# Tile 1's loads on SyncE, matmuls of ones on TensorE, and masks on GpSimd, in a fused attention and feed-forward kernel

## The chip, the cores and the metric

The kernel runs on one core of a Trainium2 chip. The metric is the device time of one execution in microseconds (us); the median of several runs is given with its range. A run comes with a mean granted TensorE clock, 1.0 being full speed. Profiles are of one execution each; their times count from the start of the profiled span. Engines: PE is TensorE (PEld its weight loads), DVE is VectorE, ACT is ScalarE, POOL is GpSimd, SP is SyncE; a q after the name marks the engine's DMA issues.

## The reference, cut to what matters

```python
# attention: q, k, v are (4 batches, 8 heads, 768, 64) in fp32
scores = q @ k.T / sqrt(64)
# heads flagged in is_retrieval: causal mask.
# other heads: causal AND (the first 4 keys OR the last 64 keys)
a = softmax(where(mask, scores, -1e9))
x = (a @ v).transpose(0, 2, 1, 3).reshape(3072, 512)
# feed-forward
h = x @ w_in          # 512 x 2048
g = h - tanh(h)
out = g @ w_out       # 2048 x 512
```

## The kernel before

The kernel cuts the 3072 tokens into 12 tiles of 256, three per batch. For each tile it casts q, k and v to 16 bits, forms scores for pairs of heads on TensorE (`sc`), exponentials on ScalarE (`pt`), masks, the product with v (`av`), the normalised result (`x`, or `x16t` from tile 3 on), its transpose (`xT`), and then the feed-forward (`ph`, `gt`, `po`, `ot`). Tiles 0 to 2 transpose their result on TensorE; tiles from 3 on do it with DMA transposes that SyncE issues. The work of one tile is laid between that of others.

A small list scheduler in the program fixes each engine's order of instructions ahead of time, from a duration that the author gives to each operation:

```python
def op(eng, ns, fn, r=(), w=(), dma=None, prio=None, port=False, after=None, behind=None): ...

def masks(threshold, key, heads, added=False):
    for h in heads:
        ...
        op("DVE", 350,
           lambda h=h, how=how: nc.vector.tensor_scalar(
               out=m4[:, h, :], in0=A4[:].rearrange("p a c -> p (a c)"),
               scalar1=threshold[:, h : h + 1], **how),          # 128 x 512, 16 bit
           r=[key, "A4", "A40", "A41", "A43"], w=[("m4", h // 2)], port=True)
...
for half in range(2):                      # tile 0: SyncE's ring, fp32
    load(0, "qk", (half,))
    load(0, "v", (half,))
...
load_cast(1, [("rv", 0, "v", 0, 1)], "qk") # tile 1: GpSimd's casting loads
if first:
    load_w_in(*W_IN[0], ())                # weights, chunk one, in GpSimd's queue
...
if t == 1 and hp == HP - 1:                # masks of tile 2, on VectorE
    fs.append(lambda: masks(thr, "thr", range(H)))
...
def st_X_tile(t):                          # tiles from 3 on: xT by DMA
    for i in range(NB):
        op("SP", 1250, lambda i=i: nc.sync.dma_start_transpose(...),
           r=[("x16t", t)], w=[("xT", t, "all", i)], dma=(512, 22.0))
```

The softmax here doesn't subtract the row's maximum and nothing guards it: scores larger than these inputs give would overflow.

## Time and profile before

| | before |
|---|---|
| time, median of 3 runs | 238.59 us (238.48 to 238.87) |
| profiled span, mean granted clock | 236.7 us, 1.00 |
| TensorE busy | 221.5 us, 94% |
| TensorE idle before its first instruction | 6.0 us |
| first feed-forward matmul of tile 0 starts | 18.93 us |
| first evacuation of a finished output block (`ot` on ScalarE) starts | 49.89 us |
| last evacuation on ScalarE starts | 230.10 us |

The last three rows are the milestones of this document: the evacuations are the same 24 instructions in every version, so the shift of the first, the sixth or the last of them tells how much time has been won or lost by then. The prediction below shows the lines that the rest of the reading of this profile rests on.

### The profile page before, as it was taken

The page shows a single profiled execution, that of the slowest core. Times are in us where ns is not written, and L with a number is a line of the kernel's source. Part 1 is how long each engine was busy: PE and PEld are TensorE (multiplying, and loading weights), DVE is VectorE, ACT ScalarE, POOL GpSimd, SP SyncE. Part 2 cuts the span into 40 slices and gives each one's busy share as a digit, 9 for nine tenths or more (in the row PEclk, how much of TensorE's full clock was granted, in tenths as well). Part 3 has the DMA queues.
Part 4 walks back from the last instruction along what each step waited for, and adds up shares of the span by engine and source line. Part 5 has one row for each costly group of instructions (what it writes and reads, how often), then busy time and mean ns, then how long its engine had stood idle before and what let it go on. Part 6 is the DMA issues. An engine that isn't in the chain of part 4 may idle for free. (4 is left out here: it accounts for less than half of the span.)

```text
span 236.7 us, 5895 instructions
## 1 busy us (share of the span) xinstructions
PE 221.5 (94%) x2220; PEld 157.8 (67%) x2220; DVE 139.0 (59%) x343; ACT 143.6 (61%) x221; POOL 90.5 (38%) x218
## 2 busy tenths in 40 slices
PE   0889899999999999999999999999999999999991
PEld 0346687756776777777676777776776777777661
DVE  1856665864488657767666655667766546443300
ACT  3668677884588387466686649537759464444320
POOL 5999420089818068480814904606300000000000
PEclk9999999999999999999999999999999999999999
DMA  5999999999997999979989695998712101310121
GB/s 128 209 140 172 204 181 204 197 228 224 206 225 182 151 248 184 227 153 206 239 168 214 136 186 130 186 171 179 134 47 66 38 31 47 90 38 9 44 89 51
DMA packets 108130, 35.29 MB, mean 149 GB/s; under 512 B 100290, under 2 KB 104642, under 8 KB 108098
## 3 DMA queue, kind: packets, MB, share of 16 engines
q1 hardware_dynamic: 92642, 28.98, 60.5%
q0 software_dynamic: 15168, 5.77, 20.7%
q8 instruction: 18, 0.29, 0.5%
q10 hardware_dynamic: 288, 0.14, 0.2%
q14 instruction: 14, 0.11, 0.2%
HBM read 27.27 MB, written 6.29 MB: 142 GB/s over the span
## 5 line engine op out<-in xcount | busy, mean ns | idle before, releaser
L1135 PE MATMUL ph<-xT,win 128*128 128x256 f16 x768 | 101.7, 273 | 0.6 <-DMA win<-in_moe_w_in_dram 0.3
L1194 PE MATMUL po<-wout,gt 128*128 128x512 f16 (+1 forms) x400 | 98.0, 371 | 0.3 <-ACT ot L1170 0.3
L1148 ACT ACTIVATE th<-ph 128x512 f32<-128x512 f32 x96 | 57.6, 601 | 59.6 <-PE ph L1135 58.2
L1155 DVE SCALAR_TENSOR_TENSOR gt<-th,ph 128x512 f16<-128x512 f32 x96 | 65.4, 684 | 44.9 <-ACT th L1148 44.4
L1135 PEld LDWEIGHTS <-win 128*128 128x128 f16 x768 | 80.0, 114 | 13.0 <-issue 1.9
L961 ACT ACTIVATE pt<-sc 128x1024 f16<-128x1024 f32 (+1 forms) x78 | 68.5, 926 | 11.4 <-PE sc L941 10.9
L1194 PEld LDWEIGHTS <-gt 128*128 128x128 f16 x400 | 36.4, 98 | 24.6 <-issue 0.9
L680 POOL CAST t<-raw_rqk 128x256 f16 x72 | 28.5, 440 | 63.3 <-DMA raw_rqk<-in_k_dram 48.1
L1030 PEld LDWEIGHTS <-pt 128*128 128x128 f16 x552 | 25.9, 98 | 10.4 <-issue 0.9
L1030 PE MATMUL av<-v,pt 128*128 128x65 f16 x304 | 26.0, 195 | 0.1
L941 PE MATMUL sc<-qk 64*128 64x128 f16 (+1 forms) x412 | 23.8, 240 | 1.7 <-DVE qk L826 1.7
L941 PEld LDWEIGHTS <-qk 64*128 64x128 f16 x412 | 13.7, 94 | 13.5 <-issue 8.9
L675 POOL CAST v<-raw_rv 128x128 f16 x72 | 21.1, 335 | 4.2 <-DMA raw_rv<-in_v_dram 4.2
L1060 DVE TENSOR_TENSOR x16t<-av,rinv 128x128 f32 x72 | 20.8, 289 | 2.3 <-DVE rinv L1050 0.3
L1030 PE MATMUL av<-vf,pt 128*128 128x65 f16 x248 | 19.6, 193 | 0.0
L1170 ACT ACTIVATE ot<-po 128x512 f32<-128x512 f32 (+1 forms) x24 | 14.3, 596 | 8.5 <-PE po L1194 8.4
L996 DVE TENSOR_TENSOR pt<-pt,m 128x1024 f16<-128x1024 f16 x16 | 12.3, 768 | 8.0 <-ACT pt L961 8.0
L1050 DVE RECIPROCAL rinv<-av 128x4 f32<-128x4 f32 x48 | 8.6, 179 | 13.4 <-PE av L1030 13.4
L986 DVE TENSOR_TENSOR pt<-pt,mS 128x512 f16<-128x512 f16 x24 | 9.8, 449 | 6.7 <-ACT pt L961 6.7
L843 PEld LDWEIGHTS <-t 128*128 128x128 f16 x48 | 3.9, 107 | 8.9 <-ACT t L644 6.8
L523 DVE TENSOR_SCALAR m<-A,thr 128x512 f16<-128x512 f16 x16 | 7.4, 501 | 1.7 <-PE sc L928 1.2
L751 POOL TENSOR_TENSOR vf<-v,rflagr 128x260 f16<-128x260 f16 x12 | 7.5, 634 | 0.0
(95 smaller groups left out, 90.8 us busy)
## 6 DMA issues: line engine op xcount, KB each, us to landing
out_dram<-ot SPq DMA_DIRECT2D x23, 256.0 KB, 2.3
raw_rqk<-in_q_dram SPq DMA_DIRECT2D x20, 256.0 KB, 4.7
raw_rqk<-in_k_dram SPq DMA_DIRECT2D x20, 256.0 KB, 4.5
raw_rv<-in_v_dram SPq DMA_DIRECT2D x18, 256.0 KB, 4.4
win<-in_moe_w_in_dram POOLq DMA_DIRECT2D x4, 512.0 KB, 8.8
wout<-in_moe_w_out_dram POOLq DMA_DIRECT2D x4, 512.0 KB, 12.4
raw_rv<-in_v_dram SPq DMA_DIRECT2D x4, 128.0 KB, 4.7
t<-in_q_dram POOLq DMA_DIRECT2D x4, 128.0 KB, 9.5
```

The costliest lines, as they stand in the source:

```text
L675: nc.gpsimd.tensor_copy(out=v1s[b]()[:, lo : lo + NB, rank : rank + 1, 0:D], in_=raw_of("v", t)[:, :, at, :],)
L680: nc.gpsimd.tensor_copy(out=t16[t % 2][:, :, :, rank : rank + 1, :], in_=raws["rqk", t][0]()[:, :, :, at, :],)
L941: nc.tensor.matmul(out=sc()[:, hh, o : o + nb * 128].rearrange("p (i c) -> p i c", c=128), lhsT=ks.rearrange("p i c -> p (i c)")[p_, jb * ...
L961: lambda pt=pt, gi=gi, wid=wid, sc=sc: nc.scalar.activation(out=pt()[:, :, 512 * gi : 512 * gi + wid], in_=sc()[:, :, 0:wid], func=AF.Exp, ...
L996: nc.vector.tensor_mul(out=pv, in0=pv, in1=m4[:, h0 : h0 + 2, 256:512].unsqueeze(2).to_broadcast([128, 2, 2, 256]),)
L1030: nc.tensor.matmul(out=av()[:, i, hh, :], lhsT=pt()[:, hh, co : co + 128], rhs=vv, start=(jb == first_jb), stop=(jb == qb),)
L1060: nc.vector.tensor_mul(out=x16s[t]()[:, :, at, :], in0=av()[:, :, hh : hh + 1, 0:D], in1=rinv()[:, :, hh : hh + 1].unsqueeze(3).to_broadca ...
L1135: nc.tensor.matmul(out=ph()[:, j, :], lhsT=w()[:, cb, c0 + fb % 4 : c0 + 512 : 4], rhs=xTs[t]()[:, cb, :], start=(cb == 0), stop=(cb == HP ...
L1148: lambda: nc.scalar.activation(out=th()[:], in_=ph()[:], func=AF.Tanh, scale=1.0 / XS),
L1155: lambda: nc.vector.scalar_tensor_tensor(out=gts[t]()[:, u * FU : (u + 1) * FU, :], in0=th()[:], scalar=-XS, in1=ph()[:], op0=ALU.mult, op ...
L1170: nc.scalar.activation(out=ot()[:, c0:c1], in_=po()[:, c0:c1], func=AF.Copy, scale=1.0 / XS)
L1194: nc.tensor.matmul(out=po()[:, c0:c1], lhsT=gts[t]()[:, f, ts * 128 : ts * 128 + 128], rhs=w_out_t[f // 4]()[:, f % 4, c0:c1], start=(f == ...
```

## The change

It has three parts. Tile 1's q and k come by SyncE's ring as fp32 in 512 B packets instead of by GpSimd's casting loads (DMA transfers that convert to 16 bits on the way), and GpSimd casts them; the weights can then be issued earlier. TensorE multiplies ones from 1.2 us until data come, and in planned gaps of tile 0, in order that its clock goes to full speed sooner. The eight masks of tile 2 go from VectorE to GpSimd. A few constants of the scheduler's cost model change with it.

```diff
@@ the scheduler
-    def run(self):
+    def run(self, fill=None, until=None):
+            if e == "PE" and t < 5600:
+                ns *= 2
...
+                idle = self.start[i] - free
+                if self.fill and idle > 200 and i != until and self.FROM < free:
+                    self.fill(int(idle * 0.5 / 107), 256)
@@ which loads take two tokens per packet (512 B)
-            return nm != "v" and t == 0
+            return nm != "v" and t < 2 and (first or not t)
@@ the ones
+            wm, key = bank([128, 512], FP32, "o", "warm")
+            def run_up(n=10, c=512):
+                for _ in range(n):
+                    nc.tensor.matmul(out=wm()[:, 0:c]..., lhsT=ones[:], rhs=ones[:]..., start=True, stop=True)
+            op("PE", 2130, run_up, r=["ones"], w=[key])
+            fillers.append(run_up)
@@ masks
-        def masks(threshold, key, heads, added=False):
+        def masks(threshold, key, heads, added=False, eng="DVE"):
-                    "DVE", 350,
-                    lambda h=h, how=how: nc.vector.tensor_scalar(
+                    eng, {"DVE": 350, "POOL": 560}[eng],
+                    lambda h=h, how=how: engs[eng].tensor_scalar(
@@ tile 1
-        load_cast(1, [("rv", 0, "v", 0, 1)], "qk")
-            load_w_in(*W_IN[0], ())
+            load(1, "qk", (0,))
+            load(1, "qk", (1,))
+            cast_qk(1, (("POOL", "POOL"), ("POOL", "POOL")))
+            load_w_in(*W_IN[0], raw_keys("q", 0, 1))
@@ masks of tile 2
-                    fs.append(lambda: masks(thr, "thr", range(H)))
+                    fs.append(lambda: masks(thr, "thr", range(H), eng="POOL"))
```

(Cut: further constants of the scheduler, the value casts of tile 0 placed earlier in the list.)

More of the change, by code (lines that the diff above doesn't have):

```diff
@@ L24 @@
     PSUM = ("sc", "m", "h", "o")
+    FROM = 5800
     RESULT = {"PE": 200, "ACT": 0, "DVE": 0, "POOL": 0, "SP": 0}
@@ L39, in op @@
                 deps.add(self.writer[k])
-            if k[0] in self.PSUM:
+            if isinstance(k, tuple) and k[0] in self.PSUM:
                 deps.update(j for j in self.readers.get(k, ()) if self.ops[j][0] != eng)
@@ L57, in op @@
         return i
-    def run(self):
+    def run(self, fill=None, until=None):
+        self.fill = fill
         n = len(self.ops)
@@ L140, in run @@
             for u in followers[i]:
-                ready[u] = max(ready[u], t + ns)
+                ready[u] = max(ready[u], free[e])
                 left[u] -= 1
@@ L147, in run @@
                 rings["POOL" if e == "POOL" else "SP"].append(
-                    [i, t + ns + (1200 if e == "POOL" else 300), each, packets * each / 16]
+                    [i, t + ns + (1200 if e == "POOL" else 1000 if t < 6000 else 400), each, packets * each / 16]
                 )
@@ L152, in run @@
         self.end = max(self.done)
+        free = self.FROM
         for i in order:
+            if self.ops[i][0] == "PE":
+                idle = self.start[i] - free
+                if self.fill and idle > 200 and i != until and self.FROM < free:
+                    self.fill(int(idle * 0.5 / 107), 256)
+                free = max(free, self.start[i] + self.ops[i][1])
+                if i == until:
+                    self.fill = None
             self.ops[i][2]()
@@ L261, in program @@
         rot = {}
+        fillers = []
         def bank(shape, dt, tag, name):
@@ L425, in program @@
             op(
-                "ACT", 400,
+                "ACT", 1150,
                 lambda: nc.scalar.dma_start(
@@ L431, in program @@
             )
-        for half in range(2):
-            load(0, "qk", (half,))
-            load(0, "v", (half,))
+        load(0, "q", (0,))
+        load(0, "k", (0,))
+        load(0, "v", (0,))
+        load(0, "q", (1,))
+        load(0, "k", (1,))
+        load(0, "v", (1,))
         if first:
             op("POOL", 204, lambda: nc.gpsimd.memset(ones[:], 1.0), w=["ones"])
+            wm, key = bank([128, 512], FP32, "o", "warm")
+            def run_up(n=10, c=512):
+                for _ in range(n):
+                    nc.tensor.matmul(
+                        out=wm()[:, 0:c].rearrange("p (a c) -> p a c", c=128), lhsT=ones[:],
+                        rhs=ones[:].unsqueeze(1).to_broadcast([128, c // 128, 128]),
+                        start=True, stop=True,
+                    )
+            op("PE", 2130, run_up, r=["ones"], w=[key])
+            fillers.append(run_up)
             op(
@@ L879, in program @@
         first_S = {}
+        first_x = []
         def near(n):
@@ L1110, in mm @@
                     )
-            op("PE", 112, mm, r=[("x16", n), "ident"], w=[key])
+            first_x.append(op("PE", 112, mm, r=[("x16", n), "ident"], w=[key]))
             op(
@@ L1262, in program @@
         cast_qk(0, (("ACT", "ACT"), ("ACT", "DVE")), (0,))
-        load_cast(1, [("rv", 0, "v", 0, 1)], "qk")
         if first:
-            load_w_in(*W_IN[0], ())
+            load(1, "qk", (0,))
+            load(1, "qk", (1,))
+            cast_qk(1, (("POOL", "POOL"), ("POOL", "POOL")))
+        else:
+            load_cast(1, [("rv", 0, "v", 0, 1)], "qk")
+        cast_v(0, ("POOL", "POOL"), (0,))
+        cast_v(0, ("POOL", "POOL"), (1,))
+        if first:
+            load_w_in(*W_IN[0], raw_keys("q", 0, 1))
             load_cast(1, (), "v")
@@ L1270, in program @@
             masks(thr, "thr", range(2 * n, 2 * n + 2), added=True)
-            st_T(n, "ACT", "DVE")
+            st_T(n, *("ACT", "DVE"))
             for f in scores(n):
                 f()
-        cast_v(0, ("POOL", "POOL"), (0,))
         cast_qk(0, (("ACT", "ACT"), ("ACT", "DVE")), (1,))
@@ L1279, in program @@
             masks(thr, "thr", range(2 * n + 4, 2 * n + 6), added=True)
-            st_T(n + 2, "ACT", "DVE")
+            st_T(n + 2, *("ACT", "DVE"))
             for f in scores(n + 2):
@@ L1283, in program @@
             st_X(n, "o", "ACT")
-        cast_v(0, ("POOL", "POOL"), (1,))
         for n in (2, 3):
@@ L1401, in program @@
         with tc.manual_schedule():
-            P.run()
+            P.run(fillers[0] if fillers else None, first_x[0])
     program(True)
```

## The prediction

> **What bounds the kernel now.** I read the page first, then the stretches by engine, then TensorE's waits, then the timeline of the first 34 us. The page's own chain is one step long and tells nothing, so the bound has to come from the others.
>
> ```profile
> span 236.7 us, 5895 instructions
> PE 221.5 (94%) x2220; PEld 157.8 (67%) x2220; DVE 139.0 (59%) x343; ACT 143.6 (61%) x221; POOL 90.5 (38%) x218
> ```
>
> TensorE is busy for 221.5 of 236.7 us: 15.2 us idle in all. Where it is idle is told by the stretches (length, then busy us of PE, PEld, DVE, ACT, POOL, then the granted clock, the DMA engines' busy us, GB/s):
>
> ```profile
> 6.00:8.00 2.00, 1.45 (x8) 0.83 (x9) 2.00 (x6) 1.27 (x3) 2.00 (x3) 1.00 1.22 272
> 10.00:12.00 2.00, 1.76 (x12) 0.88 (x14) 1.11 (x3) 1.38 (x3) 1.84 (x4) 1.00 2.28 145
> 24.00:26.00 2.00, 1.31 (x20) 0.91 (x18) 0.98 (x3) 0.78 (x2) 0.91 (x2) 1.00 1.25 207
> 60.00:100.00 40.00, 39.73 (x435) 28.88 (x434) 28.26 (x68) 28.09 (x41) 21.64 (x57) 1.00 1.06 205
> ```
>
> From 60 us to the last matmul (about 231.8) TensorE is never free for more than 0.3 us. So the time is fixed by how early TensorE gets through the work before 60 us; whatever is saved there comes off the end one for one, since the change leaves the work after tile 2 as it was. Of the idle time 6.0 us lie before the first tile, 3.1 us between 6 and 30 (24 less the busy times of twelve 2 us stretches, 20.9), 0.3 in 30 to 40, 0.7 in 40 to 60, 0.3 to 100, and the rest is the tail after the last matmul. Who is waited for up to 30 us:
>
> ```profile
> PE tp0q L843 <- ACT t L644: 6.0, 1, 6.0
> PE xp L1108 <- DVE x L1074: 1.1, 3, 0.6
> PE sc L941 <- DVE qk L826: 1.0, 2, 0.7
> PE tp0k L843 <- ACT t L644: 0.5, 1, 0.5
> PE ph L1135 <- DMA win<-in_moe_w_in_dram: 0.3, 1, 0.3
> ```
>
> The first 6.0 us are the first load and its cast. Idle time is not the only loss: early matmuls are slow, though the granted clock reads 1.00. The same pair of transposes before and after about 14.9 us, and the same mask matmuls:
>
> ```profile
> 9.31 0.39 PE L843 MATMUL tp1k<-ident,t 128*128 128x128 f16 x2
> 15.20 0.28 PE L843 MATMUL tp4q<-ident,t 128*128 128x128 f16 x2
> 7.46 1.48 PE L928 MATMUL sc<-m,ident 128*128 128x384 f16 x4
> 19.83 0.59 PE L928 MATMUL sc<-m,ident 128*128 128x512 f16 x2
> ```
>
> Four 384-column matmuls took 1.48 us, while 512 columns later add about 0.21 us each (0.59 less one latency of 0.38). All of tile 0's scores run at the slow rate.
>
> [...] The trace agrees with the halving (384 columns cost about 0.32 us each early, 128 columns 0.11), but release came only near 14.9 us, nearly 9 us after the first matmul[...]. [...] 4 to 8 us, mostly 512 B packets, moved 295 and 272 GB/s; 10 to 12 us, with GpSimd's casting loads of 256 B runs in flight, moved 145 GB/s with the engines full (those bytes are counted at the narrower destination, which explains part). [...] the mask instructions take 0.33 us at the least but one took 1.155 us, beside a GpSimd multiply from 23.29 to 24.36.
>
> **The change, part by part.**
>
> *Ones on TensorE.* Ten 512-column matmuls at the slow rate, about 0.43 us each, are 4.3 us: from about 1.2 us (the ones are set by 1.1) to 5.5, before the first real transpose at 6.0. They delay nothing. If release then comes at 5 to 8 us, tile 0 runs at full rate. Worth, on TensorE alone, between 6 and 14.9: 8 pairs of transposes x 0.11 = 0.9; 8 mask matmuls x 0.16 = 1.3; 4 score groups of 768 columns on two half arrays, about 0.16 each = 0.6; 12 value matmuls x 0.027 = 0.3; one transposed result and a 512-column mask, 0.3. Sum 3.4 us. Not all of it is on the path, so I follow the chain. The first exponential starts at 9.41. Fast, the four masks end near 8.2 instead of 8.9, the key copy on VectorE still waits for four masks there (7.46 to 7.89), so the scores run 8.0 to 8.4 and the exponential begins near 8.4: 1.0 us gained. After that VectorE carries the chain: from 7.5 it owes four key copies (1.8), four masks (1.7), a cast (0.6) and four normalisations (4 x 0.59 = 2.4), 6.5 us in all, so not done before 14.0; ScalarE from 8.3 owes a cast, two copies, four exponentials and four result copies, 0.62 + 0.88 + 3.24 + 1.48 = 6.2 us, done by 14.5. The last result copy starts at 18.62 now; with some waits I put it at 15.3, so 3.3 us gained up to the first feed-forward matmul (18.93), provided the weights are there.
>
> *Tile 1 by SyncE.* Four casting loads of 128 KB leave GpSimd (about 0.93 us of issue each, 3.7 us) and four casts of 512 columns come (about 0.61 each, as its value casts show: 2.4 us). The loads become 2048 packets of 512 B behind tile 0's on one ring instead of 4096 of 256 B beside it. Tile 0's second half should land a little sooner, tile 1's at 11 to 14 us, in time. The point that counts is the weights: the first chunk is issued at 11.13 now and can go when tile 0's second query half lands (8.3), and chunk two, issued at 15.81, can go some 3 us sooner. Now:
>
> ```profile
> 11.13 0.76 POOL L401 DMA_DIRECT2D win<-in_moe_w_in_dram  x1
> 15.81 2.24 POOL L401 DMA_DIRECT2D win<-in_moe_w_in_dram  x3
> 23.72 0.63 PE L1135 MATMUL ph<-xT,win 128*128 128x256 f16 x4 [0.30 <-DMA win<-in_moe_w_in_dram]
> ```
>
> Chunk two releases TensorE at 23.7. Read bytes ahead of its arrival: tile 0 and tile 1's q, k, v (1.57 MB each) and two chunks of 1.05 MB, 5.2 MB since about 3 us, 253 GB/s of reads. Without the bad stretch at 8 to 12 us I estimate 300 GB/s, so 20.5 us, 3.2 us sooner. Should GpSimd's casts stand ahead of it in the queue, it is 2 us.
>
> *Masks of tile 2.* Eight instructions at 0.33 to 1.16 us leave VectorE (3.7 us); on GpSimd I estimate 0.6 each from its 512-column cast, 4.8 us beside other work, in a stretch (24 to 33 us) in which it mostly waits for DMAs. On the path lies only this wait, for a key copy behind the 1.155 us mask:
>
> ```profile
> 25.04 0.40 PE L941 MATMUL sc<-qk 64*128 64x256 f16 x6 [0.69 <-DVE qk L826]
> ```
>
> Worth up to 0.7 us, of which I count 0.4, since VectorE may be blocked by GpSimd there anyway.
>
> *Sum.* The chain offers 3.3, the second chunk 2.0 to 3.2; the smaller binds, say 2.6, plus 0.4 for the masks: 3.0 us. 238.6 - 3.0 = 235.6; I say 235.5.
>
> **Rivals.**
> 1. *Weights become the bound.* TensorE is fast, but chunk two comes only 1 us sooner, since ring order or bytes hold it. For it: TensorE already waits for it, and from 11 us on DMA is what GpSimd's queue waits for (3.5 us of waits for the weights). Then the time is about 237.2.
> 2. *VectorE holds tile 0.* It is busy 2.00 of 2.00 us in 6 to 10; GpSimd's casts, now in that stretch, can lock its masks out. Against it: its total is only 6.5 us. If so, the first exponential gains 0.5 instead of 1.0 and the chain 2: about 236.8.
> 3. *Everything fits.* TensorE had 3.1 us of gaps plus 3.4 us of slow rate: 6.5 us at the very most before 30 us, 0.7 more to 60. If weights land by 19 us, 4.5 to 5 us are gained: 233.8.
> 4. *Ones in the way.* Fillers sized for half of each planned gap could stand before work that is ready earlier. A few tenths; not a loss overall.
>
> **Range and chances.** Rivals 1 and 2 give the upper side, 237.2 to 237.4; rival 3 the lower, 233.6. Faster by over 2% needs under 233.8, that is 4.8 us of at most some 7: 0.12. Slower by over 2% would need a stall that nothing in the profile suggests: 0.02. Within 2%: 0.86.
>
> **What would show it.** Transposes at 0.28 us per pair from about 7 us on; the first exponential near 8.4; the last result copy of tile 0 near 15.3; chunk two issued by 13 and landed by 20.5 to 21.5; no wait of 0.7 us for a key copy in tile 1; TensorE full after 60 us less 3. I am wrong if the slow rate lasts to 12 us, if the first feed-forward matmul waits for chunk one, or if GpSimd's queue delays the later weights so that the gain shrinks between 20 and 40 us.

## The result and the profile after

The changed kernel takes 244.26 us (243.77 to 245.07, 4 runs) against 238.73 us (238.48 to 238.87, 4 runs) for the kernel before. A ratio here is the mean time of one kernel's fast runs over that of the other's of the same rounds, so it isn't quite the ratio of the medians: 1.0236, with a 95% interval of 1.0205 to 1.0268. The change is slower by over 2%, and the prediction was 235.5 us.

The page of the changed kernel begins so (span, then busy us of each engine, share of the span, instructions):

```profile
span 242.8 us, 5927 instructions
PE 226.1 (93%) x2234; PEld 158.9 (65%) x2234; DVE 142.1 (59%) x335; ACT 142.7 (59%) x221; POOL 101.7 (42%) x226
```

The span grew by 6.1 us and TensorE's busy time by 4.6 us (226.1 less 221.5), although its real work is the same and the ones are 4.45 us ahead of the data plus a few fillers. GpSimd has 11.2 us more. The beginning went as intended. TensorE's timeline (start, us, operation, how many; in brackets the idle time before and its releaser):

```profile
1.16 4.45 PE L459 MATMUL warm<-ones 128*128 128x512 f16 x10 [1.16 <-POOL ones L454]
6.12 0.88 PE L958 MATMUL sc<-m,ident 128*128 128x384 f16 x4
8.04 0.27 PE L872 MATMUL tp1k<-ident,t 128*128 128x128 f16 x2
15.89 1.60 PE L1165 MATMUL ph<-xT,win 128*128 128x256 f16 x12
```

The four mask matmuls take 0.88 us where they took 1.48, the pair of transposes 0.27 where it took 0.39, and the first feed-forward matmul starts at 15.89 us, 3.0 us sooner than before. Then the head of the list of TensorE's waits (line, releaser: us in total, times, longest):

```profile
PE xp L1138 <- DVE x L1104: 5.0, 3, 4.5
```

The wait of 6.0 us at the top of the old list is down to 0.3, filled by ones. A new one stands in its place: a transpose of the result waits 4.5 us for VectorE. Here it is on TensorE:

```profile
41.51 1.04 PE L1224 MATMUL po<-wout,gt 128*128 128x512 f16 x4
47.04 0.29 PE L1138 MATMUL xp<-ident,x 128*128 128x128 f16 x2 [4.49 <-DVE x L1104]
47.75 1.87 PE L1165 MATMUL ph<-xT,win 128*128 128x256 f16 x8
```

The first of these lines has its like at 44.46 us in the kernel before, so TensorE was still 2.95 us ahead. The second was at 45.55 us before: the wait turned 3 us ahead into 1.5 us behind. The third is a second loss: eight such matmuls take 1.06 us elsewhere and 1.87 us here. The stretches tell why (busy us of PE, PEld, DVE, ACT, POOL, then the granted clock):

```profile
44.00:46.00 2.00, 0.00 (x0) 0.00 (x0) 2.00 (x6) 0.00 (x0) 1.22 (x1) 1.00 1.04 225
...
48.00:49.00 1.00, 1.00 (x7) 0.67 (x6) 0.58 (x2) 0.15 (x1) 0.00 (x0) 0.50 1.13 212
...
60.00:100.00 40.00, 39.15 (x421) 27.82 (x418) 26.23 (x63) 26.25 (x39) 24.50 (x63) 1.00 1.07 185
```

The last line is the long stretch after 60 us, in which TensorE is busy for 39.15 us (39.73 before): no new large loss there. While TensorE is empty, VectorE is busy without a gap. After it the granted clock is 0.50; the clock's record has it at half from 47.20 to 50.61 us, 3.41 us. What VectorE was busy with (start, us):

```profile
40.77 1.43 DVE L656 COPY mS<-mS 128x128 f16<-128x128 f16 x1
...
43.75 1.63 DVE L552 TENSOR_SCALAR m<-A,thrr 128x512 f16<-128x512 f16 x1
...
45.76 0.17 DVE L1080 RECIPROCAL rinv<-av 128x4 f32<-128x4 f32 x1
...
46.57 0.41 DVE L1104 TENSOR_TENSOR x<-av,rinv 128x256 f16<-128x256 f32 x1
```

and the same first two instructions in the kernel before:

```profile
42.30 0.18 DVE L627 COPY mS<-mS 128x128 f16<-128x128 f16 x1
...
43.11 0.35 DVE L523 TENSOR_SCALAR m<-A,thrr 128x512 f16<-128x512 f16 x1
```

A copy of 0.18 us takes 1.43 us, a mask of 0.35 us takes 1.63 us. The product with v that the reciprocal needs was done near 41.1 us, but the reciprocal stands behind these small instructions in VectorE's order and ran at 45.76 us. GpSimd, in its timeline and in its group on the page (busy us, mean ns):

```profile
32.86 12.36 POOL L552 TENSOR_SCALAR m<-A,thr 128x512 f16<-128x512 f16 x8
```

```profile
L552 POOL TENSOR_SCALAR m<-A,thr 128x512 f16<-128x512 f16 x8 | 12.4, 1556 | 0.0
```

The eight masks take 1.556 us each, not 0.6, and run back to back from 32.86 to 45.22 us. VectorE's stretched instructions end just after one of GpSimd's masks ends (40.60, 42.14, 43.68, 45.22 us): the 1.43 us copy at 42.20, the 1.63 us mask at 45.38.

The milestones give the account. Against the kernel before, the changed one is at -3.0 us at the first feed-forward matmul, +1.5 us after the wait, +3.8 us at the first evacuation (53.67 us), +4.6 us at the sixth (97.75 against 93.19) and +4.9 us at the last (235.00). From there to the end of the span it takes 7.8 us instead of 6.6. The swing from -3.0 to +3.8 us is 6.8 us; the wait (4.49 us) and the half clock (1.4 to 1.6 us, by keep_warm below) make some 6 of it, and the rest isn't traced.

### The profile page after: what moved, and what is told of

It reads as the page before. It is cut to its first block, busy times and chain, and to the rows that moved or that the text cites. A ratio compares the mean times of both kernels' runs of the same rounds, so it can differ in the third digit from the quotient of the medians.

```text
span 242.8 us, 5927 instructions
## 1 busy us (share of the span) xinstructions
PE 226.1 (93%) x2234; PEld 158.9 (65%) x2234; DVE 142.1 (59%) x335; ACT 142.7 (59%) x221; POOL 101.7 (42%) x226
## 5 line engine op out<-in xcount | busy, mean ns | idle before, releaser
L971 PE MATMUL sc<-qk 64*128 64x128 f16 (+1 forms) x412 | 23.1, 236 | 0.0
L1026 DVE TENSOR_TENSOR pt<-pt,m 128x1024 f16<-128x1024 f16 x16 | 12.8, 801 | 6.3 <-ACT pt L991 6.3
L1016 DVE TENSOR_TENSOR pt<-pt,mS 128x512 f16<-128x512 f16 x24 | 10.4, 474 | 6.3 <-ACT pt L991 6.3
L552 POOL TENSOR_SCALAR m<-A,thr 128x512 f16<-128x512 f16 x8 | 12.4, 1556 | 0.0
L1138 PE MATMUL xp<-ident,x 128*128 128x128 f16 x24 | 3.4, 221 | 5.0 <-DVE x L1104 5.0
L780 POOL TENSOR_TENSOR vf<-v,rflagr 128x260 f16<-128x260 f16 x12 | 8.0, 673 | 0.0
```

The lines of the kernel that those rows point to most:

```text
L971: nc.tensor.matmul(out=sc()[:, hh, o : o + nb * 128].rearrange("p (i c) -> p i c", c=128), lhsT=ks.rearrange("p i c -> p (i c)")[p_, jb * ...
L1026: nc.vector.tensor_mul(out=pv, in0=pv, in1=m4[:, h0 : h0 + 2, 256:512].unsqueeze(2).to_broadcast([128, 2, 2, 256]),)
```

## The experiments

Twelve kernels ran. All were correct. They went on several chips; each is compared with the runs of the kernel before on the same chip (medians 238.61, 238.68, 238.86 and 238.88 us).

### The change without the masks: undo_masks

```diff
-fs.append(lambda: masks(thr, "thr", range(H), eng="POOL"))
+fs.append(lambda: masks(thr, "thr", range(H)))
```

> The changed kernel with the masks of tile 2 back on VectorE, all else kept. Theory M (the eight GpSimd masks, 1.55 us each, hold up VectorE and so TensorE): the 4.5 us wait at 42.5 to 47.0 us and the half clock after it go away, and the 2 to 3 us gained before 32 us stay: 235.5 to 237. Rival T (tile 1 by SyncE or the ones are at fault, the masks only lie beside the loss): the time stays above 241.

Measured: 240.93 us (238.10 to 241.49), ratio 1.007 (1.0031 to 1.011). This lies between the two expected ranges. Taking this part back recovers 3.3 us by the medians (of different chips), but the other two parts don't gain. The profiled run has another wait of VectorE, of tile 0's results this time, and a half-clock stretch behind it (16.71 to 20.13 us):

```profile
16.47 0.28 PE L1138 MATMUL xp<-ident,x 128*128 128x128 f16 x2 [2.89 <-DVE x L1104]
```

VectorE had the scheduler's masks of tile 2 early, at 12.85 (1.07 us) and 13.93 (2.15 us), beside GpSimd's issues and its multiplies at 14.84 to 16.98. So VectorE's masks, 0.35 us each later in this run (at 23.89 us), were stretched beside GpSimd's work here, as its small instructions were beside GpSimd's masks before. The six runs suggest that the number of half-clock stretches varies: the runs of clock 0.988 to 0.991 took 240.9 to 241.5 us, those of 0.997 and 0.999 took 238.1 and 239.9 us.

### The masks alone: only_masks

The kernel before with the masks of tile 2 on GpSimd (the diff above in reverse, with the `eng` argument).

> The kernel before with nothing changed but the masks of tile 2 on GpSimd. Theory M: slower by 4 to 8 us, 243 to 247, with eight GpSimd instructions of 1.55 us and a TensorE wait of over 3 us near 45 us. Rival T: within 1 us of the kernel before, 238 to 239.5.

Measured: 242.37 us (239.96 to 243.17), ratio 1.0134 (1.0087 to 1.018). The part costs 3.8 us by itself, a little less than Theory M said, and by another way than it said. Here the order placed the masks of 1.57 to 1.59 us each between GpSimd's DMA issues, so that these went out late, and TensorE waited for them:

```profile
PE po L1194 <- DMA wout<-in_moe_w_out_dram: 2.7, 1, 2.7
PE av L1030 <- DMA v<-in_v_dram: 1.0, 1, 1.0
```

The masks end by 39.42 us here, and VectorE's small instructions behind them, from 40.20 us on, run at their usual length (the copy 0.18 us, the mask 0.35 us). A half-clock stretch follows (48.61 to 52.02 us). The first evacuation is 3.8 us late and the last 4.1 us: a loss before 50 us goes through to the end whole.

### The ones alone: only_ones

The kernel before with `run_up` and the fillers in gaps.

> The kernel before with the ones on TensorE and the fillers alone. If the clock of tile 0 is worth what the first 16 us of the two traces suggest: 1.5 to 2.5 us faster, 236.2 to 237.2, the first feed-forward matmul near 17 instead of 18.9. If tile 0 is held by VectorE and by tile 1's loads all the same: under 0.7 us, 238 or more.

Measured: 240.83 us (239.66 to 241.86), ratio 1.0108 (1.0086 to 1.0129). In the profiled run the clock went full at 3.94 us, and half again from 10.77 to 14.18 us, over the gaps of tile 0 (full from 14.95 in the kernel before). Fillers of half of each planned gap did not hold it. The order also changed with the cost model's rule for early matmuls: GpSimd issued weights two to four at 17.42 us, not 15.81. The runs have clocks of 0.98 to 0.993, so by an estimate from these means most have two or three half-clock stretches (one of 3.41 us at half in 238 us takes 0.007 off the mean). The ones alone, with the order that came with them, lose.

### Tile 1's loads alone: only_tile1

The kernel before with tile 1 on SyncE and the scheduler's new constants.

> The kernel before with tile 1 by SyncE's ring and the new constants and order of the plan alone (no ones, no GpSimd masks). If the weights bind: chunk two lands some 2 us sooner but TensorE is slow until 15 us: 0.5 to 1.5 us faster, 237.2 to 238.2. If this part is at fault for the loss: 240 or more.

Measured: 243.3 us (238.92 to 245.27), in two groups: four of six runs are slow, with clocks of 0.979 to 0.985, and the verdict is "unclear" (ratio of the two fast runs 1.0164, 1.0119 to 1.0208). Why four were slow isn't known; none of them was profiled. The profiled run is the quickest, 238.92 us, without a half-clock stretch, and it shows where its gain went. Its first evacuation came 2.6 us earlier than before (47.26 us); its sixth, that of tile 3, only 0.24 us earlier. Between them stands this wait for the transposed result of tile 3:

```profile
79.37 1.06 PE L1151 MATMUL ph<-xT,win 128*128 128x256 f16 x8 [2.43 <-DMA xT<-x16t]
```

So in this one run the part wins 2.6 us by 50 us, and something at tile 3 takes them.

### Half of the masks on each engine: half_masks

```diff
-fs.append(lambda: masks(thr, "thr", range(H), eng="POOL"))
+fs.append(lambda: masks(thr, "thr", range(H // 2), eng="POOL"))
+fs.append(lambda: masks(thr, "thr", range(H // 2, H)))
```

> The changed kernel with only heads 0 to 3 of tile 2's masks on GpSimd, 4 to 7 on VectorE. Theory P (while a GpSimd mask of 1.55 us runs, VectorE's instructions[...] wait for its end; the last four masks, 39.05 to 45.25 us, starve the ranking of the heads and what stands behind it): the four end near 39, before most of the ranking, the 4.5 us wait of TensorE goes, and the time is 2.5 to 4 us under the changed kernel, 240 to 241.8. Rival D (VectorE waits for the data of the masks, heads 2 and 3[...]): these are made at the same time as before, so the wait and the time stay, 243.5 to 245.

Measured: 239.57 us (239.10 to 240.30), ratio 1.0027 (0.9995 to 1.0058), 4.7 us under the full change. GpSimd's four masks run from 33.48 to 39.68 us, done before VectorE's small instructions at 40 us. The wait of 4.5 us and the half clock are gone; the clocks of all runs are 0.993 to 0.999. In the full change the masks that the waiting heads need were done by 39.06 us, so a late mask can't have caused its wait; VectorE's stretched instructions (a copy of 0.18 us took 1.43 us, a mask of 0.35 us took 1.63 us) remain as the cause. A late mask has a price of its own, though: here VectorE waits 1.89 us for the data of one before its multiply at 38.17 us, and TensorE 1.22 us, to 40.00 us, for what stands behind it. One rival is untested: the scheduler planned with 560 ns for a GpSimd mask, and no run gave it the true 1556, with which it might have found a harmless place for all eight. Yet the kernel is no faster than before. Its first evacuation is 1.1 us early, its sixth 0.65 us late, and at tile 3 it waits too:

```profile
80.26 1.06 PE L1165 MATMUL ph<-xT,win 128*128 128x256 f16 x8 [1.74 <-DMA xT<-x16t]
```

### Ones in the gap: keep_warm

The full change with 18 more matmuls of ones placed just ahead of the transpose that waits 4.5 us.

```diff
+def keep_warm():
+    kw = ps.tile([128, 2, 512], FP32, tag="sc", bufs=bufs["sc"], name="keep")
+    for _ in range(18):
+        nc.tensor.matmul(out=kw[:, 0, :]..., lhsT=ones[:], rhs=ones[:]..., start=True, stop=True)
```

> The changed kernel with 18 matmuls of ones, 512 columns each, put before the transpose that TensorE waits 4.5 us for. If the 3.4 us at half clock after that wait are a loss of their own: the record of the clock shows no half at 47 to 51 us and the time is 1.3 to 2 us under the changed kernel, 242.3 to 243. If that loss is hidden behind other waits: within 0.5 us of 244.3.

Measured: 243.66 us (242.44 to 245.85), ratio 1.0186 (1.0137 to 1.0234), between the two expected ranges. In the profiled run no half clock follows the gap: the eight matmuls take 1.03 us, the first evacuation comes at 52.31 us, 1.36 us sooner than in the full change, and at 113 us it is still 1.6 us ahead. This run then had a half-clock stretch at 116.02 to 119.44 us, behind a wait of 1.90 us for transposed data, so it ended late; the run with a clock of 0.997 took 242.44 us. The half clock after the wait is thus a loss of its own, some 1.4 to 1.6 us, and its return depends on the run.

### The order in SyncE's queue, a first try: sp_order

only_tile1 with tile 6's key and value loads put behind tile 3's transposes in SyncE's queue.

> Tile 1 by SyncE alone, as before, with one instruction moved in SyncE's queue: the load of tile 6's first keys goes behind the transposes of tile 3's result, as in the kernel before, and not ahead of them. Theory Q (the 2.6 us won by 50 us are given back at tile 3, because its transposed result comes through SyncE's queue and DMA engines that are full): TensorE's wait there, 2.4 us, falls to about 1 or less, and a run without a second half-clock stretch ends 1 to 1.5 us sooner, near 237.5 against 238.9. Rival: the transposes of tile 3 are held by the DMA engines' load alone, the wait stays at 2 us or more and the time within 0.5 us of before's.

Measured: 242.09 us (239.55 to 243.81; one run slow), ratio 1.0095 (1.0042 to 1.0148). The run that was profiled had a wait of 2.73 us for VectorE at 17.97 us and a half-clock stretch to 23.59 us, so it had no early gain that tile 3 could have taken. This tells nothing of the queue; the question needs a kernel with a stable beginning, which half_masks is.

### What GpSimd's operations cost: pool_ops

The kernel before with pairs of 128x512 instructions added at the end of GpSimd's program, one look: 238.56 us.

> The kernel before with six GpSimd instructions of 512 columns, twice each, at its end, into tiles that nobody reads: what a mask costs there by itself. If the threshold read from memory is what is slow: z_ptr 1.55 us, z_imm with the threshold in the instruction near 0.6. If the comparison in 16 bit is slow: z_imm 1.55 too and the multiplication near 0.6. If every tensor_scalar is: z_mul 1.55 as well, only the copy z_copy near 0.45 to 0.6, the product of two tensors z_tt near 1.0.

The groups (busy us, mean ns):

```profile
L1411 POOL TENSOR_SCALAR z_ptr<-A,thr 128x512 f16<-128x512 f16 x2 | 3.1, 1564 | 0.1
...
L1414 POOL TENSOR_SCALAR z_imm<-A 128x512 f16<-128x512 f16 x2 | 3.0, 1482 | 0.0
L1424 POOL TENSOR_TENSOR z_tt<-A 128x512 f16<-128x512 f16 x2 | 2.1, 1032 | 0.0
L1423 POOL COPY z_copy<-A 128x512 f16<-128x512 f16 x2 | 1.2, 602 | 0.0
```

The price lies in the kind of instruction: each of the four tensor-scalars tried costs 1.5 to 1.6 us, with its scalar from memory (z_ptr) or immediate (z_imm), as a multiply (1.614 us) and in 32 bits (1.486 us). A copy of the same size costs 0.60 us and a product of two tensors 1.03 us. The cast that the prediction took as its stand-in is of the cheap kind.

### Tile 6's loads behind tile 3's transposes: half_sp_all, half_sp, before_sp_all

These three ran together on one chip. half_sp_all is half_masks with all of tile 6's loads behind the transposes, half_sp with its keys and values only, and before_sp_all is the kernel before with the edit of half_sp_all, as a control.

```diff
+turned = {}
 ...
-                op(                                  # st_X_tile
+                turned[t] = op(
 ...
                             after=gated if first and t == 1 else first_S[t * HP + hp],
+                            behind=turned.get(3) if t == 4 else None,    # half_sp: ... if t == 4 and hp
```

> half_masks (four masks on GpSimd, four on VectorE) with one more edit: SyncE issues all loads of tile 6 after the two transposes of tile 3, instead of three or four of them before. In half_masks the eighth result of tile 3 was ready at 72.6 us, its transposes were issued at 74.73 us behind a store and a key load, and TensorE sat idle 1.74 us for them, up to 80.26 us (in the kernel before the same matmul starts at 78.75 us without a wait). Theory Q (the gain is clipped at tile 3 because the transposes stand behind tile 6's loads in SyncE's queue and share the DMA engines with them): the transposes are issued by 73 us, the wait falls under 0.5 us, the first feed-forward matmul of tile 3 starts at 77.5 to 78.5 us, the evacuation that came at 93.84 us comes at 91.5 to 92.5 us, and the time falls from 239.57 us to about 237.5 to 238.3 us, a little under the kernel before. Rival R (the store's data, the softmax or the other waits of tile 3 take the place of this wait, or a later tile waits for the delayed loads): the wait at tile 3 goes, but the end stays at 239 to 240 us, with a new wait after 85 us.

> half_masks with only the key and value loads of tile 6 moved behind tile 3's transposes in SyncE's queue; tile 6's query loads stay ahead of them and go on using the DMA engines. Theory Q in the form 'order in the queue': same as with all of the loads moved, 237.5 to 238.5 us. In the form 'full DMA engines': the transposes are issued about 0.5 us earlier only (the queue is held by the query loads up to 73 us) and land late; the wait stays at 1 to 1.5 us and the time at 239 us.

> The kernel before with the same move (all loads of tile 6 behind tile 3's transposes), a control. In the kernel before the transposes were issued as soon as the result was ready (73.86 to 73.92 us) and the feed-forward did not wait for them. If Q is right, nothing is gained here: 238.2 to 239.2 us. If this edit is worth as much here as in half_masks (over 0.8 us), then it is a better schedule by itself and says nothing on the clipped gain.

| kernel | time, us | ratio to before | tile 3's result ready | transposes issued | first feed-forward matmul of tile 3 | sixth evacuation |
|---|---|---|---|---|---|---|
| before | 238.86 | | 73.86 | 73.92 | 78.75 | 93.19 |
| half_masks | 239.57 | 1.0027 (0.9995 to 1.0058) | 72.62 | 74.73 | 80.26, after 1.74 us | 93.84 |
| half_sp | 239.46 | 1.0019 (0.9993 to 1.0045) | 72.45 | 73.42 | 79.25, after 1.34 us | 93.30 |
| half_sp_all | 237.50 (237.41 to 237.71) | 0.9938 (0.9913 to 0.9962) | 72.36 | 72.42 | 77.67, no such wait | 91.68 |
| before_sp_all | 238.68 | 0.9987 (0.9962 to 1.0011) | | | | 93.24 |

(half_masks is from another chip; its time was taken against 238.68 us there. The profile times of before are those shown above.) SyncE's timeline in half_masks and then in half_sp_all shows what moved:

```profile
70.49 2.46 SPq L342 DMA_DIRECT2D raw_rqk<-in_q_dram  x2
73.05 1.09 SPq L1212 DMA_DIRECT2D out_dram<-ot  x1
74.19 0.43 SPq L342 DMA_DIRECT2D raw_rqk<-in_k_dram  x1
74.73 3.63 SPq L1118 DMA_TRANSPOSE xT<-x16t  x2
```

```profile
69.97 1.05 SPq L1213 DMA_DIRECT2D out_dram<-ot  x1
72.42 3.42 SPq L1119 DMA_TRANSPOSE xT<-x16t  x2
75.89 1.20 SPq L342 DMA_DIRECT2D raw_rqk<-in_q_dram  x2
```

In half_masks the result is ready at 72.62 us, but the queue is in the midst of two query loads whose issue takes 2.46 us, then come a store and a key load. With all of tile 6's loads moved the transposes go 0.06 us after the result, and the wait on TensorE is gone. With the query loads left ahead (half_sp) they end at 72.13 us, a store follows that they had held back, the transposes still go 1.0 us late, and most of the wait and all of the time remain. So the query loads are the ones that count, by themselves and by the store behind them. How much of their effect is the place in the queue and how much the bytes in front of the transposes on the DMA engines, these runs don't part. In the kernel before the same edit changes nothing, since there the result came later than the queue was free. So it isn't a better order in itself: it only lets an earlier result through. half_sp_all is faster than both kernels: by 0.6% than the kernel before (its ratio; the interval is clear of 1), and by 2.8% than the changed one (237.50 against 244.26 us, on different chips).

### The repaired kernel without the ones: no_ones

half_sp_all without `run_up` and the fillers, each engine's planned order otherwise unchanged.

> half_sp_all without the ones: neither the ten matmuls ahead of the first data nor those in the gaps of tile 0; everything else in the same order on each engine. Theory W (the ones are worth what the prediction said once the masks and tile 3 no longer take it back): the full clock comes at 9 to 15 us instead of 6, tile 0 is done about 1 to 1.5 us later, nothing downstream clips that, and the time rises from 237.5 to 238.5 to 239 us. Rival V (the ones bring nothing: waits for data or for VectorE between 10 and 30 us end last anyway, or tile 0's gaps bring the half clock back with and without them): 237.2 to 238.0 us.

Measured: 238.25 us (237.41 to 239.69), ratio 0.9962 (0.9911 to 1.0012). The intervals of the two overlap and the best runs are equal, so this doesn't settle whether the ones are worth the 0.7 us between the medians. The profiles say why it can't be much: without ones the clock is full only from 13.12 us, but the first feed-forward matmul starts at 17.08 us; with them TensorE gets there sooner and then waits 0.76 us for the first chunk of weights, up to 16.58 us (half_sp_all). By the last evacuation the runs are 0.33 us apart. And the profiled run with ones had its clock at half again from 16.67 to 20.08 us.

## Why the prediction was wrong

In short: the step that failed is the one on the masks, "0.6 each" and "4.8 us beside other work", counted as a gain of 0.4 us. They took 1.556 us each, not beside VectorE's work but in its way, and TensorE waited 4.49 us for VectorE. The step "one for one" failed too, as half_masks and half_sp_all show.

**The ones.** Right in its effect on tile 0: the clock was full from 6.24 us (said: 5 to 8, an estimate that nothing in the trace of the kernel before had shown), the first exponential at 8.76 us (said: 8.4), the last result copy at 15.92 us (said: 15.3, before 18.62), the first feed-forward matmul 3.0 us sooner. In the 3.41 us before 6.24 us TensorE was busy for 3.09 us. The view of the granted clock doesn't show the slow start: it reads 1.00 from the beginning of the span, while in the kernel before a pair of transposes took 0.37 to 0.42 us until 14.95 us, where the clock's record begins, and 0.28 us after it. What the steps left out is that the full clock can be lost again. It was, after the gap that began at 42.55 us here and inside tile 0 in only_ones, each time for 3.41 us.

**Tile 1 by SyncE.** Right on chunk two: issued at 12.08 us (said: by 13) and TensorE released by it at 21.59 us (said: 20.5 to 21.5, so 0.1 us late).

**The masks.** The step "on GpSimd I estimate 0.6 each from its 512-column cast, 4.8 us beside other work" failed in three ways. The instruction costs 1.556 us, so 12.4 us; pool_ops shows that the cast is not a stand-in for a tensor-scalar. The masks ran at 32.86 to 45.22 us and not at 24 to 33, since GpSimd's order has weight and value issues ahead of them that waited for room (the last weight issue at 30.25 us). And this work does not lie beside VectorE's: the prediction had seen a mask of 1.155 us beside a GpSimd multiply, and counted this only as a cap on a gain of 0.4. GpSimd's eight masks of 1.556 us stood in a row against a row of small VectorE instructions, which came to their ends at 42.20 and 45.38 us, just after the ends of two masks (42.14 and 45.22 us), about one group of them per mask. On the path that was 4.49 us, where a gain of 0.4 had been written. half_masks, in which the masks end before 40 us, removes it and 4.7 us of the time.

**The clock after a wait.** No step has it. The gap of 4.49 us was followed by 3.41 us at half rate. By keep_warm this costs another 1.4 to 1.6 us. Together with the wait it is some 6 us of the way from 3.0 us of lead to 3.8 us of lag.

**"Whatever is saved there comes off the end one for one."** True of losses: 3.8 us at 50 us became 4.1 us at the end in only_masks. Wrong of gains: 2.6 us at 50 us became 0.24 us at tile 3 in only_tile1, and half_masks, which has neither the long wait nor a half clock, was no faster than before. The sentence rested on TensorE's having no idle time after 60 us. That says that nothing else limits TensorE at its present pace, not that nothing stands close behind: tile 3's transposes were issued in a queue that was just free in time (73.86 and 73.92 us). half_sp_all clears it, and then the gain is the same at the first evacuation (1.57 us) and at the last (1.51 us).

**The rivals.** None of the four holds the wait. Rival 2 had GpSimd hold up VectorE, but in tile 0 and by casts (in the kernel before, a mask of VectorE that starts at 8.99 us beside a cast of GpSimd takes 0.76 us, the shortest 0.33). "A stall that nothing in the profile suggests" was in the profile's own line of a 1.155 us mask beside a GpSimd multiply of 1.07 us; beside GpSimd's masks of 1.556 us, which I hadn't priced, the same kind of mask took 1.63 us.

**What is left of the predicted 3.0 us.** half_sp_all gains 1.4 us in time (238.86 less 237.50). Of the 3.0 us at the first feed-forward matmul it has 2.35 us (16.58 against 18.93), held by the first chunk of weights; its profiled run lost some of the rest to a half-clock stretch at 16.67 us. About 0.8 us more go at the very end, in every profiled run that has the tile 1 part and that I looked at: from the last evacuation to the end of the span 7.3 to 7.8 us pass, in those without it 6.4 to 6.7 us. In the two that I followed to the last instruction (before and half_sp_all) the last store lands 2.0 us after its issue in both, but the closing sequence after it takes 2.0 us in one and 2.8 us in the other. SyncE's last waits come in another order there: before, four of them are already over when the store lands; in half_sp_all all of them still come after. I tried nothing on this.

**Why runs of one kernel differ.** This is a reading of the traces after the fact; no run was made to test it. The record of the clock changes at multiples of 3.41 us within a run (in the changed kernel full from 6.24 us, half from 47.20 us, twelve times 3.41 us later, and full again from 50.61 us), from a start that differs between runs. I laid windows of 3.41 us on that grid and read TensorE's busy time in each. The seven windows ahead of the last matmuls that end in a return to half clock hold 0.16 us (the changed kernel), 0.52 (undo_masks), 1.09 (only_masks), 1.51 (keep_warm), 1.86 (sp_order), 1.93 (only_ones) and 2.00 us (half_sp_all). Busy time alone doesn't sort them from the others: the full clock was kept over windows of 2.16 us (the changed kernel, 40.38 to 43.79 us) and 2.18 us (half_sp), but also over 1.77 us (undo_masks, 78.15 to 81.57 us), 1.79 us (only_tile1, 77.75 to 81.16 us) and 1.82 us (the kernel before, 229.99 to 233.40 us). What the latter three lack is transposes on TensorE. With these left out, the seven windows hold at most 1.51 us, and of all windows of the fourteen profiles that kept the full clock each holds at least 1.52 us, but for one of 1.31 us in only_ones, the first after a release. That sorting was found afterwards in these traces, and its margin is thin; what the clock really counts stays open. Half_masks and half_sp_all run the same program up to 60 us, and their lines can be read each on its own grid. First half_masks on its grid, then half_sp_all (busy us of PE first, then the other engines and the granted clock):

```profile
11.65:15.06 3.41, 2.38 (x36) 1.44 (x36) 2.32 (x8) 2.60 (x6) 3.26 (x5) 1.00 1.20 210
15.06:18.47 3.41, 2.25 (x26) 1.77 (x23) 0.90 (x4) 2.34 (x5) 3.29 (x6) 1.00 1.78 188
```

```profile
13.26:16.67 3.41, 2.00 (x30) 1.16 (x30) 2.09 (x7) 2.83 (x6) 3.41 (x6) 1.00 1.57 198
```

In half_sp_all the window with the gaps, the longest of them 0.76 us, holds 2.00 us of work and the half clock follows at 16.67 us. In half_masks 13.26 to 16.67 us holds even less, 1.92 us, but that is no window of its grid: the gaps fall half into one and half into the next, with 2.38 and 2.25 us, and the clock stays. So a half clock followed a window here that was far from empty. That the place of the grid, which the program didn't set, decided which of the two runs paid is a reading of this one pair.

**Still open.** Whether the ones pay at all, what the scheduler would do with the true price of a GpSimd mask, what the clock counts as work, and whether the grid's start could be steered.

## What to carry to other kernels

Moving work to an idle engine needs two prices: what the instruction costs there, taken from the same kind of instruction and not from a cheaper one (a mask took 1.556 us on GpSimd, a copy of its size 0.60), and whom it holds up while it runs (here a copy of 0.18 us on VectorE took 1.43 us). An unbroken busy engine downstream does not mean that an earlier start comes off the end: look for the next gate (a queue in order, a buffer, a transfer) whose slack is smaller than the gain, and move it with the change. A stretch with gaps on TensorE cost more than the gaps here, since in some runs 3.41 us at half clock followed it (1.4 to 1.6 us of loss, by keep_warm), so versions are best judged with the granted clock of each run beside its time.
